# A Fourier factor as four 64x64 tiles of TensorE instead of one block-diagonal 128x128 product

## The chip, the cores and the metric

The kernel runs on one core of one Trainium2 chip. The metric is the device time of one execution in microseconds (us). Most executions agree within 0.3%. Each variant was run several times on a chip beside runs of the kernel before on the same chip. A ratio below is the mean time of a kernel's fast runs over the mean of the other kernel's fast runs of the same rounds, so it isn't quite the ratio of the medians that stand beside it.

Before the change: 3389.97 us (median of three runs, 3387.17 to 3390.71); with the fourth run, which was made beside the changed kernel (3380.72 us), the median is 3388.57 us.

## The reference, cut to what matters

Eight sequences of 3008 tokens with 256 features go through a Fourier filter along the tokens, then each token through a layer of 2048 hidden units with ELU. All in float32.

```python
X = np.fft.rfft(x, axis=1)                 # x: (8, 3008, 256)
Y = X * (filt_r + 1j * filt_i)[None]
y = np.fft.irfft(Y, n=3008, axis=1)
h = y.reshape(24064, 256) @ w_in           # (256, 2048)
g = np.where(h > 0, h, np.exp(np.minimum(h, 0)) - 1)
out = g @ w_out                            # (2048, 256)
```

## The kernel before

3008 = 47 * 64. A token is n = 47 * n2 + n1, and n1 = 24 * h + i with h = 0 or 1. The first factor, a product over n2 (64 values), is done for both halves h at once: h = 0 lies on partitions 0 to 63, h = 1 on 64 to 127, and the table `wa` is block-diagonal, so half of the 128x128 product multiplies by zeros. `psa` is its result in PSUM, `t1` the copy in SBUF (both are on-chip memories), and `z_move` carries `t1` to `t2`, where n1 lies on the partitions. The second factor (`psb`), the filter, and the way back (`psi`, `psn`) follow.

```python
XC = 4                                     # values of i in a chunk; 6 chunks a batch
def a_unit(b, i):                          # two values of i
    c, r = divmod(i, XC // 2)
    ...
    nc.tensor.matmul(ps, wa, xs[b, c][:, 2 * r:2 * r + 2, :], start=True, stop=True)
    nc.scalar.activation(out=t1s[b, c][:, 2 * r:2 * r + 2, :], in_=ps, func=AXT.Copy)

def z_move(b, c):                          # 16 moves of 32 partitions x 1 KB
    ...
    for h in range(2):
        for ri in range(2):
            p0 = h * 64 + ri * 32
            r0 = ri * SL + h * H + c * XC
            for n in range(XC):
                nc.sync.dma_start(t2s[b][r0 + n:r0 + n + 1, :, :], t[p0:p0 + 32, n, :])
```

The layer's work is laid out in slots, 96 a batch. One matmul call leaves two passes in the trace. In each slot TensorE does `up` (4 passes of 512 columns into `ph`) and `down` (8 passes of 256 columns into `po`). The mixing of batch b is put between the slots of batch b - 1: `a_unit` in slots 2, 6, 10 ... 46, `b_unit` from slot 52. Batch 0 is mixed with no layer work beside it; this is the head of the trace.

## Time and profile before

| what | value | view |
|---|---|---|
| span of the profiled run | 3384.2 us | page |
| TensorE busy | 91% | page, engine shares |
| psa | 192 passes, 108.3 us busy | page, groups |
| first pass of the layer (ph) | at 320.0 us | timeline |
| period of a batch (first psb to first psb, mean of six) | 389.3 us | timeline |
| a slot without mixing | 3.44 us | timeline |
| what a psa pair adds to its slot | 0.86 us | timeline |

On TensorE the printed duration of a pass isn't its cost: a psa pass of 592 ns is followed by the next after 429 ns. The cost is the distance from its start to the next start. The lines themselves are shown in the prediction.

### The profile page before, as it was taken

How to read it: one execution, taken by the hardware profiler on the slowest of the kernel's cores; microseconds unless marked ns; L12 is line 12 of the kernel's file. 1: busy time of each engine (PE TensorE's matmuls, PEld its weight loads, DVE VectorE, ACT ScalarE, POOL GpSimd, SP SyncE). 2: the span in 40 equal slices, each digit the busy share in tenths (PEclk: the TensorE clock that was granted, in tenths of full speed). 3: DMA queues.
4: the chain of work that ended last, by engine and by line, in shares of the span. 5: the costliest groups of instructions: out<-in, count | busy, mean ns of one | idle time of the engine just before them, and what ended most of it. 6: DMA issues, size and time to landing. Idle time of an engine off the chain costs nothing.

```text
span 3384.2 us, 30459 instructions
## 1 busy us (share of the span) xinstructions
PE 3075.4 (91%) x11200; PEld 2079.4 (61%) x11200; DVE 1494.1 (44%) x2241; ACT 663.5 (20%) x1137; POOL 171.6 (5%) x148
## 2 busy tenths in 40 slices
PE   1234999999989999999999999899999999999999
PEld 0122666666666666666666666576666666666666
DVE  0185337333553336433473336433373335533343
ACT  0001221222212222222212222122212222122121
POOL 0010002000010001000020001100020000100000
PEclk9656999999999999999999999999999999999999
DMA  7321111102110121101210121102111021100000
GB/s 116 60 82 42 44 36 35 29 19 49 34 37 11 38 43 34 28 17 42 46 34 17 25 48 36 35 13 43 37 35 29 19 50 21 38 10 12 7 13 12
DMA packets 101653, 116.43 MB, mean 34 GB/s; under 512 B 29928, under 2 KB 79848, under 8 KB 101232
## 3 DMA queue, kind: packets, MB, share of 16 engines
q1 hardware_dynamic: 96768, 99.73, 13.9%
q10 hardware_dynamic: 4000, 11.67, 1.3%
q0 software_dynamic: 736, 3.09, 0.8%
q8 instruction: 88, 1.44, 0.2%
q14 instruction: 61, 0.50, 0.1%
HBM read 39.39 MB, written 24.64 MB: 19 GB/s over the span
## 4 chain that ended last, share of the span: by engine, by line
PE 75%; SPq 14%; DMA 7%; DVE 2%; issue 1%; ACT 1%; ACTq 0%; DVEq 0%
PE po L244 34%; PE ph L226 34%; SPq L208 14%; DMA t<-t 4%; PE psn L215 3%; PE psa L158 2%; PE psb L177 1%; DMA wai<-wai_t 1%; PE psi L195 1%; DMA wd<-in_moe_w_out_dram 1%; DMA wd<-in_moe_w_in_dram 0%; SPq L171 0%; DMA out_dram<-o 0%; ACT g L231 0%; ACT t L197 0%
## 5 line engine op out<-in xcount | busy, mean ns | idle before, releaser
L244 PE MATMUL po<-w_out,g 128*128 128x256 f32 x6144 | 1466.0, 382 | 33.8 <-ACT o L248 33.8
L226 PE MATMUL ph<-y,w_in 128*128 128x512 f32 (+1 forms) x3072 | 1425.5, 587 | 32.3 <-DVE g L232 32.2
L244 PEld LDWEIGHTS po<-w_out,g 128*128 128x128 f32 x6144 | 1170.6, 191 | 428.1 <-issue 261.4
L230 DVE TENSOR_SCALAR g<-ph 128x512 f32<-128x512 f32 (+1 forms) x768 | 522.1, 680 | 1040.6 <-PE ph L226 1037.6
L231 ACT ACTIVATE g<-g 128x512 f32<-128x512 f32 (+1 forms) x768 | 475.9, 620 | 2001.2 <-DVE g L230 2001.2
L226 PEld LDWEIGHTS ph<-y,w_in 128*128 128x128 f32 x3072 | 585.5, 191 | 436.4 <-issue 357.0
L232 DVE SCALAR_TENSOR_TENSOR g<-g,ph 128x512 f32<-128x512 f32 (+1 forms) x768 | 519.7, 677 | 665.1 <-ACT g L231 665.1
L188 POOL TENSOR_TENSOR s<-s,s 128x512 f32<-128x512 f32 x128 | 163.9, 1281 | 1237.0 <-DVE s L187 1192.7
L195 PE MATMUL psi<-s,wi 128*96 128x256 f32 x512 | 143.5, 406 | 72.4 <-DVE s L187 50.8
L158 PE MATMUL psa<-xc,wa 128*128 128x512 f32 x192 | 108.3, 655 | 98.6 <-DMA xc<-in_x_dram 98.6
L197 ACT ACTIVATE t<-psi 96x512 f32<-96x512 f32 x128 | 75.4, 589 | 582.0 <-DMA t<-t 499.6
L177 PE MATMUL psb<-t,wb 96*128 96x256 f32 x512 | 142.7, 404 | 44.9 <-DMA t<-t 33.5
L195 PEld LDWEIGHTS psi<-s,wi 128*96 128x96 f32 x512 | 87.9, 174 | 152.7 <-issue 111.7
L183 DVE TENSOR_TENSOR s<-psb,filt 64x512 f32<-64x512 f32 x128 | 86.6, 677 | 147.7 <-PE psb L177 147.2
L177 PEld LDWEIGHTS psb<-t,wb 96*128 96x128 f32 x512 | 103.1, 204 | 74.5 <-issue 47.5
L215 PEld LDWEIGHTS psn<-wai,t 128*128 128x128 f32 x768 | 102.5, 196 | 65.2 <-issue 65.2
L158 PEld LDWEIGHTS psa<-xc,wa 128*128 128x128 f32 x192 | 37.4, 207 | 142.6 <-issue 142.6
L215 PE MATMUL psn<-wai,t 128*128 128x128 f32 x768 | 103.0, 279 | 21.9 <-DMA t<-t 21.9
L187 DVE TENSOR_TENSOR s<-psb,filt 64x512 f32<-64x512 f32 x128 | 89.0, 695 | 1.8
L184 DVE SCALAR_TENSOR_TENSOR s<-psb,filt 64x512 f32<-64x512 f32 x128 | 88.7, 693 | 1.7
L186 DVE TENSOR_TENSOR s<-psb,filt 64x512 f32<-64x512 f32 x128 | 87.5, 684 | 1.7
L146 POOL MEMSET xc<- 64x256 f32 x8 | 2.4, 306 | 1522.3 <-PE psa L158 1450.6
(26 smaller groups left out, 264.3 us busy)
## 6 DMA issues: line engine op xcount, KB each, us to landing
t<-t SPq DMA_DIRECT2D x768, 32.0 KB
t<-t SPq DMA_DIRECT2D x1024, 24.0 KB
out_dram<-o SPq DMA_DIRECT2D x184, 128.0 KB
xc<-in_x_dram SPq DMA_DIRECT2D x88, 256.0 KB
wd<-in_moe_w_in_dram ACTq DMA_DIRECT2D x8, 512.0 KB
wd<-in_moe_w_out_dram ACTq DMA_DIRECT2D x16, 256.0 KB
wb<-wb_t ACTq DMA_DIRECT2D x1, 1536.0 KB
wi<-wi_t ACTq DMA_DIRECT2D x1, 1536.0 KB
```

Source lines behind the costliest of these rows:

```text
L158: nc.tensor.matmul(ps, wa, xs[b, c][:, 2 * r:2 * r + 2, :], start=True, stop=True)
L177: nc.tensor.matmul(ps[:, u, :], wb[:, k, :], t2s[b][:, k, :], start=True, stop=True)
L187: nc.vector.tensor_tensor(out=s2[hi], in0=ps[hi], in1=f[lo], op=ALU.mult)
L188: nc.gpsimd.tensor_tensor(out=s1, in0=s1, in1=s2, op=ALU.add)
L195: nc.tensor.matmul(ps[0:KR, u, :], wi[:, 2 * i + u, :], s[:, u, :], start=True, stop=True)
L208: nc.sync.dma_start(t4s[b][p0 + u:p0 + u + 1, :, :], t[r0:r0 + H, u, :])
L215: nc.tensor.matmul(ps[:, ts(q, P)], t4s[b][:, 4 * m + q, ds(dh * P, P)], wai, start=True, stop=True)
L226: nc.tensor.matmul(ph[:, 0:w], w_in[:, dt, ts(jt, P)], ys[b, m][:, dt, 0:w], start=(dt == 0), stop=(dt == 1))
L230: nc.vector.tensor_scalar(out=g[:, 0:w], in0=ph[:, 0:w], scalar1=0.0, scalar2=None, op0=ALU.min)
L231: nc.scalar.activation(out=g[:, 0:w], in_=g[:, 0:w], func=AXT.Exp)
L232: nc.vector.scalar_tensor_tensor(out=g[:, 0:w], in0=g[:, 0:w], scalar=1.0, in1=ph[:, 0:w], op0=ALU.subtract, op1=ALU.max)
L244: nc.tensor.matmul(po[q // 2][:, q % 2, :], g[:, ts(q, P)], w_out[:, jt, :], start=(jt == 0 and q % 2 == 0), stop=(jt == JT - 1 and q % 2 ...
```

## The change

The intent is to leave out the multiplications by zero. The array is used as four independent tiles of 64x64. A tile takes half h as its rows, and writes to the partitions of g: g = 0 for the first two values of i of the chunk, g = 1 for the other two. The four calls of a chunk go to four different tiles. `t1` is therefore laid out by g on the partitions, and `z_move` reads it so; a_units move from twelve half-visits to six visits a batch.

```diff
-    def a_unit(b, i):
-        c, r = divmod(i, XC // 2)
-        ...
-        ps = psM.tile([P, 2, D], FP32, tag="mx", name="psa")
-        nc.tensor.matmul(ps, wa, xs[b, c][:, 2 * r:2 * r + 2, :], start=True, stop=True)
-        nc.scalar.activation(out=t1s[b, c][:, 2 * r:2 * r + 2, :], in_=ps, func=AXT.Copy)
+    def a_unit(b, c):
+        t1s[b, c] = t1p.tile([P, XC, D], FP32, tag="t1", name="t1")
+        ps = [psM.tile([P, 2, D], FP32, tag="mx", name="psa%d" % h) for h in range(2)]
+        for g in range(2):
+            for h in range(2):
+                r, o = slice(h * 64, h * 64 + 64), slice(g * 64, g * 64 + 64)
+                nc.tensor.matmul(ps[h][o], wa[r, r], xs[b, c][r, 2 * g:2 * g + 2, :], start=True, stop=True)
+        for h in range(2):
+            nc.scalar.activation(out=t1s[b, c][:, 2 * h:2 * h + 2, :], in_=ps[h], func=AXT.Copy)
@@ z_move
-                p0 = h * 64 + ri * 32
-                    nc.sync.dma_start(..., t[p0:p0 + 32, n, :])
+                    p0 = n // 2 * 64 + ri * 32
+                    nc.sync.dma_start(..., t[p0:p0 + 32, 2 * h + n % 2, :])
@@ plan
-            for i in range(2 * NXC):
-                s = t + 2 + 4 * i
+            for c in range(NXC):
+                s = t + 6 + 8 * c
```

(The rest of the diff takes comments out.)

More of the change, by code (lines that the diff above doesn't have):

```diff
@@ L151, in x_load @@
             nc.sync.dma_start(t[h * 64:h * 64 + 64, 0:w, :], rows[:, lo:lo + w, :])
-    def a_unit(b, i):
-        c, r = divmod(i, XC // 2)
-        if r == 0:
-            t1s[b, c] = t1p.tile([P, XC, D], FP32, tag="t1", name="t1")
-        ps = psM.tile([P, 2, D], FP32, tag="mx", name="psa")
-        nc.tensor.matmul(ps, wa, xs[b, c][:, 2 * r:2 * r + 2, :], start=True, stop=True)
-        nc.scalar.activation(out=t1s[b, c][:, 2 * r:2 * r + 2, :], in_=ps, func=AXT.Copy)
+    def a_unit(b, c):
[7 more added lines that the diff above has]
+            nc.scalar.activation(out=t1s[b, c][:, 2 * h:2 * h + 2, :], in_=ps[h], func=AXT.Copy)
     def z_move(b, c):
@@ L167, in z_move @@
             for ri in range(2):
-                p0 = h * 64 + ri * 32
                 r0 = ri * SL + h * H + c * XC
                 for n in range(XC):
-                    nc.sync.dma_start(t2s[b][r0 + n:r0 + n + 1, :, :], t[p0:p0 + 32, n, :])
+                    p0 = n // 2 * 64 + ri * 32
+                    nc.sync.dma_start(t2s[b][r0 + n:r0 + n + 1, :, :], t[p0:p0 + 32, 2 * h + n % 2, :])
     def b_unit(b, i):
@@ L328 @@
             t = (b - 1) * PER
-            for i in range(2 * NXC):
-                s = t + 2 + 4 * i
-                at(s, a_unit, b, i)
-                if i % 2 == 1:
-                    c = i // 2
-                    at(s, z_move, b, c)
-                    nb, nxt = (b, c + 2) if c + 2 < NXC else (b + 1, c + 2 - NXC)
-                    if nb < B:
-                        at(s, x_load, nb, nxt)
+            for c in range(NXC):
+                s = t + 6 + 8 * c
+                at(s, a_unit, b, c)
+                at(s, z_move, b, c)
+                nb, nxt = (b, c + 2) if c + 2 < NXC else (b + 1, c + 2 - NXC)
+                if nb < B:
+                    at(s, x_load, nb, nxt)
             for i in range(NB):
```

## The prediction

> **What bounds the kernel now.** I first read the page: the engine shares, then the chain that ended last.
>
> ```profile
> span 3384.2 us, 30459 instructions
> ...
> PE 3075.4 (91%) x11200; PEld 2079.4 (61%) x11200; DVE 1494.1 (44%) x2241; ACT 663.5 (20%) x1137; POOL 171.6 (5%) x148
> ...
> PEclk9656999999999999999999999999999999999999
> ...
> PE 75%; SPq 14%; DMA 7%; DVE 2%; issue 1%; ACT 1%; ACTq 0%; DVEq 0%
> PE po L244 34%; PE ph L226 34%; SPq L208 14%; DMA t<-t 4%; PE psn L215 3%; PE psa L158 2%; PE psb L177 1%; DMA wai<-wai_t 1%; PE psi L195 1%; DMA wd<-in_moe_w_out_dram 1%; DMA wd<-in_moe_w_in_dram 0%; SPq L171 0%; DMA out_dram<-o 0%; ACT g L231 0%; ACT t L197 0%
> ...
> ```
>
> TensorE bounds it, at 0.9 or more of its clock except in a cold head (the first four slices). The product that changes, psa at L158, is 2% of the chain. But shares over the whole span mix stages, so I asked where psa runs. By stretches: its first 24 records lie in the first 130 us (batch 0, no layer work yet), then 24 records in each of seven stretches of some 165 us, one per batch. For one of these (1105 to 1293 us) I read the waits and TensorE's groups, and then a piece of its timeline.
>
> ```profile
> POOL xc L146 <- PE psa L158: 219.3, 1, 219.3
> ACT g L231 <- DVE g L230: 146.0, 50, 3.6
> ...
> PEld psa L158 <- issue: 4.3, 18, 0.2
> ...
> L158 PE MATMUL psa<-xc,wa 128*128 128x512 f32 x24 | 12.3, 593 | 0.0
> ...
> 1119.42 1.88 PE L226 MATMUL ph<-y,w_in 128*128 128x512 f32 x4
> 1121.14 1.02 PE L158 MATMUL psa<-xc,wa 128*128 128x512 f32 x2
> 1122.00 1.89 PE L244 MATMUL po<-w_out,g 128*128 128x256 f32 x8
> 1123.73 1.88 PE L226 MATMUL ph<-y,w_in 128*128 128x512 f32 x4
> 1125.44 1.89 PE L244 MATMUL po<-w_out,g 128*128 128x256 f32 x8
> ```
>
> The reader is to see three things. No TensorE group idles in this stretch (0.0 before psa), and no wait ends on TensorE waiting for another engine, so a microsecond added or removed there moves the end by a microsecond. Second, one matmul call leaves two records (96 calls, 192 records; weights, pass, weights, pass). Third, the cost of a pass is its distance to the next start, not its printed length: psa takes 1122.00 - 1121.14 = 0.86 us for two, 0.43 us each, while its mean length is 593 ns. The 0.16 us between them is the pipeline's tail, hidden today behind the next pass. The chain of this stretch agrees: it charges 0.86 us to each psa pair.
>
> **What the Trainium skill says.** (1) "TensorEngine Tiling (Array Packing)", section Key Properties: tiles execute independently, but a change of tiling mode drains TensorE. The kernel before shows no such drain: its passes follow each other at 0.43 us, even between products of 96 and 128 rows (psb at 904.72, the next at 905.59). (2) "TensorE: Matmul & The Clock Gate", section "Part 3: Packing small matmuls — row/col tiling": products on different tiles start some 4 ns apart, but matmuls start and end strictly in program order. No run here has tiles yet. (3) The same page, "Back-to-back issue gap", gives N / 2.4 + 2.5 ns, 216 ns for 512 columns; here the measured 0.43 us is twice that, and I use the measurement. (4) The tiling page, "Gotcha 1: PSUM Pressure": different row tiles must not share a bank. The change obeys it (one bank for each half h).
>
> **The change part by part.**
>
> *Removed:* per chunk of four i, two calls of 128x128 by 512 columns: 4 passes x 0.43 = 1.72 us. There are 8 x 6 = 48 chunks, of which 42 (batches 1 to 7) lie in the TensorE-bound stretches: 72 us.
>
> *Added:* per chunk, four calls of 64x64 by 512 columns in the order (h0,g0), (h1,g0), (h0,g1), (h1,g1), each on its own tile: 8 passes of 512 columns. A pass keeps its 512 columns, so I keep 0.43 us for it. The intent is that all four run at once: 2 passes deep, 0.86 us per chunk, half of before.
>
> I doubt that, because of the two passes. Program order is A1 A2 B1 B2 C1 C2 D1 D2, where A2 needs the tile of A1. If starts are in program order (point 2), A2 starts when A1's columns are through, B1 at once beside A2; B2 waits for B1 and C1 goes beside B2; and so on. It is a staircase: five steps, not two: 5 x 0.43 = 2.15 us, 0.43 more than before.
>
> *The two mode switches.* Each chunk goes from the full array to tiles and back, amid layer work. At each, the tail of 0.16 us (593 less 430 ns) is no longer hidden. The first weights of the new mode may also be unable to load ahead; a weight load of 128 columns lasts 190 ns in this trace. So 0.16 to 0.35 us a switch, as an estimate; I take 0.25, 0.5 us per chunk.
>
> *Sum:* 2.15 + 0.5 = 2.65 us against 1.72, so +0.93 us a chunk, times 42 = +39 us.
>
> *Beside other work, so free:* ScalarE's copies stay 96 of some 0.58 us, and two now follow each other; with the exponential of a slot (0.63 us) that is 1.8 us of a 3.44 us slot (1125.44 - 1122.00). They reach across both halves, but the shapes are unchanged. The moves after it keep their count (96 a batch) and size (32 partitions by 1 KB); only the half they read from alternates. The plan moves the even a_units from slots 2, 10, ... to 6, 14, ...; psn at slots 2, 18, 34 no longer shares a slot with psa, which frees nothing on a full TensorE. In the head, psa waits for the DMA of x (98.6 us over six waits) and does not appear on the chain at all; at the cold clock four psa passes span 3.75 us, so an added step is below 1 us, partly hidden: 0 to +2 us. I take 0.
>
> The last move of a batch has room. In this stretch its last issue is at 1283.6 us and the first psb is at 1294.33, some 10 us later. A longer psa delays both alike; a shorter one takes at most 6 x 0.86 = 5 us from the gap. SyncE waits 73.9 us for ScalarE's copies in this stretch, so the queue isn't full either.
>
> So the centre of my leading reading is 3390 + 39 = 3429 us. I shade it by 4 us for the chance that the tiles do better: 3425.
>
> **The rivals.**
>
> *All four tiles at once.* If a blocked second pass holds up only its own tile and not the queue, a chunk takes 0.86 us, plus 0.3 to 0.7 for the switches: 1.2 to 1.6, so -0.5 to -0.1 us a chunk, -21 to -5 us: 3369 to 3385. Even with free switches it is 42 x 0.86 = 36 us, 1.1%, so 2% faster is out of reach. For it: the tiling page calls tiles independent, and the banks are laid out for it. Against: the pair of passes per call, plain in the counts, and the order of starts. Chance 0.25.
>
> *Tiles one after another.* If f32 passes don't overlap across tiles at all, it is 8 x 0.43 = 3.44 us, plus 0.2 to 0.5 for the switches: +1.9 to +2.2 us a chunk, +80 to +92 us: 3470 to 3482, slower by 2.4 to 2.7%. For it: the f32 pass takes twice the skill's figure, so it uses the array or its inputs differently from the case that was measured there. Against: nothing in this trace; it has no tiles. Chance 0.17.
>
> *A staircase with weight loads in it.* Today a pass's weights load during the pass before (the load at 1120.71, its pass at 1121.14). If the load for a new tile can't start until the pass ahead of it in the program starts, each of the three handovers waits for a load of up to 0.19 us: 2.65 + 3 x 0.19 = 3.22 us, +1.5 us a chunk, +63 us: 3453. Chance 0.2; the plain staircase keeps 0.38.
>
> *The end moves to the DMA queue.* If the first factor gets faster, the moves of t1 may end after psb wants them. The 10 us of room speak against it; it would only cut the gain of the first rival.
>
> **Range and chances.** Batches are alike to a few us, so the spread is that of the mechanism, not of the runs (3387 to 3391). The four readings give 3369 to 3482 us. A range of 3370 to 3475 us leaves out the best corner of the first and half of the serial one. 2% faster (3322) is beyond even the free case: 0.01. 2% slower starts at 3458 us: the serial reading, and part of the loaded staircase if its switches cost more than I took: 0.22. Within 2%: 0.77.
>
> **What would show each step.** In the changed profile psa should have 384 records of 64 rows by 512 columns. From the start of the first psa pass to the start of the po pass after it: near 2.6 us for the staircase, 1.2 to 1.6 us for full overlap, 3.6 us or more for none. Within a chunk the eight starts tell it directly: in the staircase, starts come in pairs 0.43 us apart (A2 with B1, B2 with C1, C2 with D1). The switches show as more than 0.43 us from the last ph start to the first psa start, and from the last psa start to the first po. The exact change of the period of a batch (389 us now) times seven should be the change of the time. The prediction is wrong if psa spans 0.9 us (switches free and tiles together), if a TensorE wait for ScalarE's copies or for a psM buffer appears in the stretch, or if psb starts waiting for the moves.

## The result, and the profile after

The changed kernel takes 3368.38 us (median of four, 3365.12 to 3369.85); the ratio to the kernel before is 0.994 (95% interval 0.9926 to 0.9954). It is 20 us faster than the median of all four runs before, where the prediction had 35 us slower; the time lies 1.6 us under the range on record.

From the page of the changed kernel (the span, the engine shares and the groups of the new product):

```profile
span 3366.1 us, 30866 instructions
...
PE 3058.7 (91%) x11392; PEld 2050.8 (61%) x11392; DVE 1495.1 (44%) x2241; ACT 663.2 (20%) x1137; POOL 171.8 (5%) x148
...
L160 PE MATMUL psa<-xc,wa 64*64 64x512 f32 x384 | 69.2, 673 | 100.4 <-DMA xc<-in_x_dram 100.4
...
L160 PEld LDWEIGHTS psa<-xc,wa 64*64 64x64 f32 x384 | 12.3, 140 | 150.5 <-issue 127.8
...
```

The group of the old product on the page before:

```profile
L158 PE MATMUL psa<-xc,wa 128*128 128x512 f32 x192 | 108.3, 655 | 98.6 <-DMA xc<-in_x_dram 98.6
```

There are twice the passes of psa (384), and yet they keep TensorE busy for less time, 69.2 us against 108.3 us. A pass lasts no less (673 ns, before 655 ns), so the passes must lie side by side.

The timeline of TensorE in a stretch of the TensorE-bound stage (start, duration, line, product, number of passes):

```profile
1115.18 1.88 PE L229 MATMUL ph<-y,w_in 128*128 128x512 f32 x4
1116.99 1.09 PE L160 MATMUL psa<-xc,wa 64*64 64x512 f32 x8
1118.01 1.99 PE L247 MATMUL po<-w_out,g 128*128 128x256 f32 x8
1119.84 0.59 PE L229 MATMUL ph<-y,w_in 128*128 128x512 f32 x1
```

The slot with psa lasts 1119.84 - 1115.18 = 4.66 us (the same in all 42 such slots), a slot without 3.44 to 3.45 us. A chunk thus costs 1.21 us, against 2 x 0.86 = 1.72 us before: 0.51 us saved, times 42 chunks of batches 1 to 7 = 21 us. Eight passes take 1.02 us to the start of po. The same view up to 1117.1 us has four of them:

```profile
1116.99 0.66 PE L160 MATMUL psa<-xc,wa 64*64 64x512 f32 x4
```

Record by record in the packed trace, the eight starts are four at 1116.992, 1116.999, 1117.005 and 1117.012, and four at 1117.472 to 1117.492. All four tiles work together, twice; the experiments below test this reading.

In the same stage the waits (who waited for whom; us in total, times, longest) are as before: none of TensorE's own matmuls waits for another engine.

```profile
POOL xc L146 <- PE psa L160: 216.7, 1, 216.7
ACT g L234 <- DVE g L233: 142.9, 50, 3.2
...
PEld psa L160 <- issue: 4.5, 6, 0.8
...
```

The 18.1 us between the two profiled runs fall as follows, from the first starts of products in both traces.

| stretch | before, us | after, us | difference |
|---|---|---|---|
| start to the first ph (head) | 320.0 | 324.5 | +4.5 |
| first ph to the first psb of batch 1 | 195.4 | 192.5 | -2.9 |
| from there to the first psb of batch 7 (six batches) | 2335.8 | 2314.6 | -21.2 |
| from there to the last start | 527.8 | 529.3 | +1.5 |

The seven stages with psa give -24.1 us; psa itself gives 21 of them. As to the rest, TensorE's idle time before ph fell from 32.3 to 28.2 us; why was not followed up. The head's +4.5 us is taken up below.

### The profile page after: what moved, and what is told of

The parts are those of the page before. It is cut to its first block, busy times and chain, and to the rows that moved or that the text cites. A ratio compares the mean times of both kernels' runs of the same rounds, so it can differ in the third digit from the quotient of the medians.

```text
span 3366.1 us, 30866 instructions
## 1 busy us (share of the span) xinstructions
PE 3058.7 (91%) x11392; PEld 2050.8 (61%) x11392; DVE 1495.1 (44%) x2241; ACT 663.2 (20%) x1137; POOL 171.8 (5%) x148
## 4 chain that ended last, share of the span: by engine, by line
PE 74%; SPq 15%; DMA 6%; DVE 2%; issue 1%; ACT 1%; ACTq 0%; POOL 0%; DVEq 0%; POOLq 0%
PE po L247 34%; PE ph L229 33%; SPq L211 15%; DMA t<-t 4%; PE psn L218 3%; PE psb L180 1%; PE psa L160 1%; DMA wai<-wai_t 1%; PE psi L198 1%; DMA wd<-in_moe_w_out_dram 1%; DMA wd<-in_moe_w_in_dram 0%; SPq L174 0%; DMA out_dram<-o 0%; ACT g L234 0%; ACT t L200 0%
## 5 line engine op out<-in xcount | busy, mean ns | idle before, releaser
L229 PE MATMUL ph<-y,w_in 128*128 128x512 f32 (+1 forms) x3072 | 1428.3, 587 | 28.2 <-DVE g L235 28.2
L160 PE MATMUL psa<-xc,wa 64*64 64x512 f32 x384 | 69.2, 673 | 100.4 <-DMA xc<-in_x_dram 100.4
L160 PEld LDWEIGHTS psa<-xc,wa 64*64 64x64 f32 x384 | 12.3, 140 | 150.5 <-issue 127.8
```

What stands on the lines that cost most here:

```text
L160: nc.tensor.matmul(ps[h][o], wa[r, r], xs[b, c][r, 2 * g:2 * g + 2, :], start=True, stop=True)
L229: nc.tensor.matmul(ph[:, 0:w], w_in[:, dt, ts(jt, P)], ys[b, m][:, dt, 0:w], start=(dt == 0), stop=(dt == 1))
```

## The experiments

All kernels gave the reference's result. The table has the medians and the ratios to the kernel before; the runs of it on the same chip had medians of 3383.15 us (first four rows), 3385.53 us (next three), 3386.5 us (next four) and 3386.7 us (last three). The medians of before_again and before_look count one slow run each; their fast runs alone have 3388.67 and 3385.25 us.

| run | median, us | ratio (95%) |
|---|---|---|
| before_again | 3389.72 | 1.0016 (1.0001 to 1.0031) |
| after_again | 3363.52 | 0.9939 (0.9925 to 0.9952) |
| split_same | 3366.43 | 0.9949 (0.9935 to 0.9963) |
| split_turn | 3365.75 | 0.9946 (0.9933 to 0.996) |
| switch_twice | 3380.16 | 0.9985 (0.9971 to 0.9999) |
| paired | 3356.14 | 0.9909 (0.9896 to 0.9923) |
| moves_by_source | 3350.83 | 0.9894 (0.9881 to 0.9908) |
| before_look | 3385.43 | 0.9998 (0.9984 to 1.0013) |
| before_moves | 3370.63 | 0.9953 (0.9942 to 0.9965) |
| moves_far | 3323.41 | 0.9815 (0.9802 to 0.9828) |
| paired_moves | 3344.43 | 0.9878 (0.9866 to 0.9891) |
| two_tiles | 3399.61 | 1.0045 (1.003 to 1.0059) |
| before_far | 3344.61 | 0.9884 (0.987 to 0.9898) |
| paired_far | 3318.27 | 0.9801 (0.9789 to 0.9814) |

### Controls: before_again, after_again, before_look

No edit. Expected of before_again:

> The unchanged kernel before against itself: the noise of the ratio, and a second profile of its head. All theories: ratio 1.000 within 0.3%. If the head's end is a matter of the program, its first ph pass starts at 320 us again (within 1 us); if it is scatter of the DMA, it moves by several us, and then the 4.6 us by which the changed kernel's first ph starts later (324.5) is no part of the change.

Expected of after_again:

> The changed kernel unchanged, as the control of this call. All theories: 0.994 of the kernel before, 0.992 to 0.996. Its first ph pass at 324.5 us again if the later head belongs to the change, anywhere from 318 to 326 if it is scatter.

Expected of before_look:

> The unchanged kernel again, for a profile of its head in the fast state (the last one fell into a state four times slower). Changed kernels so far had their first ph at 320.8 to 324.5 us, the kernel before at 320.0 once. If the head is not of the change, this one lies between 318 and 325 as well; if the change costs the head some 2 us, it is at 320 or below. Time ratio 1.000 within 0.3%.

The changed kernel repeats its gain (0.9939). Its first ph pass came at 320.9 us this time, not 324.5: most of the later head of the first profile is scatter. The other variants with one of the two old orders of moves have it at 320.8 to 322.3 us. The kernel before has one fast profile of its head (320.0 us), and a loss of 1 or 2 us there isn't excluded. The ratio of before_again is 0.16% off 1, so differences under 0.2% are not read below.

### Does a pass that waits for its tile hold up the others? split_same, split_turn

The prediction's staircase rests on this. In split_same each call of 512 columns becomes two calls of 256 on the same tile, one right behind the other; in split_turn the same eight calls take turns over the tiles.

```diff
+                for u in range(2):            # split_same: inside g, h
-                nc.tensor.matmul(ps[h][o], wa[r, r], xs[b, c][r, 2 * g:2 * g + 2, :], ...)
+                    nc.tensor.matmul(ps[h][o, u, :], wa[r, r], xs[b, c][r, 2 * g + u, :], ...)
```

```diff
+        for u in range(2):                    # split_turn: outside g, h
```

> The changed kernel, with each tile's 512 columns in two calls of 256 right behind each other, so that in the program every second call needs a tile that is busy. Theory 1 (a pass that waits for its tile is passed by later passes for free tiles): four rounds of 0.215 us, 0.86 us as now, chunk 1.0 to 1.1 us from the first psa start to po; time that of the changed kernel within 0.3% (3368, up to 3376 with a few hundredths more per round). Theory 2 (only the two passes of one call are laid apart, a call that waits for its tile holds up the calls behind it, the staircase of the prediction one level up): ten steps of 0.215 us, 2.15 us, +1.29 us a chunk over 42 chunks: +54 us, 3422.

> The same eight calls of 256 columns, but taking turns: four tiles, then the four tiles again. Theory 1 and theory 2 alike: no call waits for a tile behind which others could go, 0.86 us of rounds, time of the changed kernel within 0.3%. If this is as slow as split_same, the cost is of the number of calls, not of their order.

Both run at the time of the changed kernel (0.9949 and 0.9946 against 0.9939). The timeline of TensorE in split_same:

```profile
1114.12 1.88 PE L230 MATMUL ph<-y,w_in 128*128 128x512 f32 x4
1115.93 1.11 PE L161 MATMUL psa<-xc,wa 64*64 64x256 f32 x16
1116.98 1.99 PE L248 MATMUL po<-w_out,g 128*128 128x256 f32 x8
1118.81 1.88 PE L230 MATMUL ph<-y,w_in 128*128 128x512 f32 x4
```

Sixteen passes in 1.05 us to po, and 1118.81 - 1114.12 = 4.69 us for the slot, 0.03 us more than with four calls. A staircase of ten steps, with whole calls kept in order, would have shown 2.15 us; with single passes kept in order it is thirteen steps, 2.80 us. Record by record, the starts come in four rounds of four, 0.22 to 0.27 us apart. So later calls pass over calls that wait for a tile. In split_same the first pass for the fourth tile has twelve passes ahead of it in the program; three of them had started on the other tiles, and nine were passed over. The price is small: starts within a round are 13 ns apart, and 7 ns in split_turn.

The head of the changed kernel shows the same in another way. There the second half of x comes late. Three views of TensorE's timeline, up to 9.4 us, 13.3 to 13.5 us, and 14.25 to 14.4 us:

```profile
8.43 1.94 PE L160 MATMUL psa<-xc,wa 64*64 64x512 f32 x2 [8.43 <-DMA xc<-in_x_dram]
...
13.40 1.12 PE L160 MATMUL psa<-xc,wa 64*64 64x512 f32 x3 [3.04 <-DMA xc<-in_x_dram]
...
13.40 1.98 PE L160 MATMUL psa<-xc,wa 64*64 64x512 f32 x6 [3.04 <-DMA xc<-in_x_dram]
```

Both passes of the first call run alone at 8.43 us (0.88 us apart; the kernel before has 0.85 us in its head, at a granted clock of 0.50 from 97 to 102 us). The second call needs the other half of x, and everything waits for it, also the third call, whose data is there: a wait for data holds up the queue. When it ends at 13.40 us, three passes start within 13 ns, and the last three 0.91 us later. No fixed order of the eight starts explains both this and the stage above. Here the second pass of the first call ran before the first pass of the second call; there four tiles started before any second pass. The records don't name their tile; but the two passes of one call were 0.88 us apart where they ran alone, so three that start within 13 ns are on three tiles. Which unit deals the passes out isn't in the trace.

### Passes on one tile: two_tiles

The upper left and the lower right tile alone do all the work, two calls each, in the program order h = 0, 0, 1, 1. The layout and the moves are those of the kernel before, with four banks and four copies a chunk.

```diff
-        for g in range(2):
-            for h in range(2):
-                r, o = ...
-                nc.tensor.matmul(ps[h][o], wa[r, r], xs[b, c][r, 2 * g:2 * g + 2, :], ...)
+        for h in range(2):
+            r = slice(h * 64, h * 64 + 64)
+            ps = [psM.tile([P, 2, D], FP32, tag="mx", ...) for g in range(2)]
+            for g in range(2):
+                nc.tensor.matmul(ps[g][r], wa[r, r], xs[b, c][r, 2 * g:2 * g + 2, :], ...)
+            for g in range(2):
+                nc.scalar.activation(out=t1s[b, c][r, 2 * g:2 * g + 2, :], in_=ps[g][r], ...)
```

> The same products on two tiles alone (upper left and lower right), two calls one after the other on each, program order h0, h0, h1, h1, four banks and four copies of 64 partitions a chunk; layout and moves of the kernel before. Theory (a visit costs the passes that fall on one tile, 0.43 us each, plus 0.35 us): 4 x 0.43 + 0.35 = 2.07 us a chunk, +0.86 us over 42 chunks: +36 us against the changed kernel, 3400 to 3404, slower than the kernel before by 14. If the strict order of starts of my prediction held, h1 would start only beside the second h0 call: six steps, 2.93 us, 3438. If the two tiles shared a limit of f32 streaming: eight steps, 3474.

```profile
1122.27 1.88 PE L229 MATMUL ph<-y,w_in 128*128 128x512 f32 x4
1124.08 1.94 PE L160 MATMUL psa<-xc,wa 64*64 64x512 f32 x8
1125.95 1.99 PE L247 MATMUL po<-w_out,g 128*128 128x256 f32 x8
1127.78 0.59 PE L229 MATMUL ph<-y,w_in 128*128 128x512 f32 x1
```

This is TensorE's timeline again. The slot lasts 5.51 us, so a chunk costs 2.07 us, as worked out from four passes of 0.43 us on each tile. The time, 3399.61 us, is at the low end of where this theory put it. With whole calls kept in order a chunk would have cost 2.93 us, six steps; with single passes in order, as the prediction had it, it is seven steps, 3.36 us (the expectation counts six). The packed records also mark the passes that end a call: the pair at 1124.562 and 1124.575 us does, so it is the second passes of the first and the third call, and the third call had started both its passes before the second call started its first (1124.99 us). The same tables and the same zeros left out, but on two tiles, lose 0.45% against the block-diagonal product. The gain of the change is the working together of four tiles.

### What a visit to the tiles costs: switch_twice, paired

In switch_twice each chunk is done in two visits four slots apart, 256 columns on four tiles each time; the copies stay together. In paired two chunks are done in one visit, in slots 6, 22 and 38.

```diff
-                at(s, a_unit, b, c)
+                at(s - 4, a_unit, b, c, 0)    # switch_twice: ps[h][o, u, :] for u = 0
+                at(s, a_unit, b, c, 1)        # then u = 1 and the copies
```

```diff
-            for c in range(NXC):
-                s = t + 6 + 8 * c
+            for c2 in range(0, NXC, 2):       # paired
+                s = t + 6 + 8 * c2
+                for c in (c2, c2 + 1):
+                    at(s, a_unit, b, c)
+                for c in (c2, c2 + 1):
+                    at(s, z_move, b, c)       # and x_load as before
```

> The changed kernel with each chunk's columns in two visits four slots apart (four tiles of 256 columns each time): the streamed columns stay, the mode switches double. Theory (what keeps the chunk at 1.21 us instead of 0.86 is paid per visit: 0.09 us going in, 0.09 us and 0.10 us coming out, 0.05 us between the rounds): +0.28 to +0.35 us a chunk over 42 chunks, +12 to +15 us against the changed kernel, 3380 to 3383. Rival (it is paid per streamed column, passes in tiles being slower): no difference, 3368 within 3 us. My prediction's own 0.25 us a switch would make it +21 us.

> The changed kernel with two chunks in one visit (slots 6, 22, 38), half as many switches. Theory of a cost per visit: 3 visits fewer a batch, 21 in batches 1 to 7, 0.28 to 0.35 us each: -6 to -7 us, 3361 to 3362. Rival per column: no difference. Rival that the moves come late (32 moves at once, all four psM buffers taken): psb or psn waits, slower than 3368.

TensorE's timeline, first of switch_twice, then of paired:

```profile
1117.36 1.88 PE L233 MATMUL ph<-y,w_in 128*128 128x512 f32 x4
1119.17 0.66 PE L162 MATMUL psa<-xc,wa 64*64 64x256 f32 x8
1119.76 1.99 PE L251 MATMUL po<-w_out,g 128*128 128x256 f32 x8
1121.59 1.88 PE L233 MATMUL ph<-y,w_in 128*128 128x512 f32 x4
```

```profile
1109.94 1.88 PE L229 MATMUL ph<-y,w_in 128*128 128x512 f32 x4
1111.75 1.95 PE L160 MATMUL psa<-xc,wa 64*64 64x512 f32 x16
1113.62 1.99 PE L247 MATMUL po<-w_out,g 128*128 128x256 f32 x8
1115.46 1.88 PE L229 MATMUL ph<-y,w_in 128*128 128x512 f32 x4
```

Take the slot's 3.44 to 3.45 us and the columns (0.215 us for 256, 0.43 us for 512, times the passes on one tile) from the distance of the ph starts:

- switch_twice: 4.23 - 3.445 - 2 x 0.215 = 0.355 us a visit.
- changed kernel: 4.66 - 3.445 - 2 x 0.43 = 0.355 us a visit.
- paired: 5.52 - 3.445 - 4 x 0.43 = 0.355 us a visit.
- two_tiles: 5.51 - 3.445 - 4 x 0.43 = 0.345 us a visit, with two tiles only.
- kernel before: 4.30 - 3.445 - 2 x 0.43 = about 0 us, with no tiles.

The cost is paid per visit, not per column or per tile. That it is a drain at the change of mode is the likely reading; no run shows the drain itself. In the changed kernel it lies at four places, from the starts of the records: 0.09 us before the first psa pass, 0.05 us between the two rounds, 0.09 us before the first po pass, and 0.10 us between the first two po passes (0.32 us apart, where it is 0.215 us elsewhere); the 0.02 us left are the starts of one round, 7 ns apart. The times follow: switch_twice is 0.46% slower than the changed kernel's control, some 16 us (expected 12 to 15), and paired is 0.3% faster, some 10 us (expected 6 to 7; the last few us aren't certain). In the traces the seven stages with psa are 8 us shorter than in the changed kernel.

### The moves on the way: moves_by_source, before_moves, moves_far, paired_moves, before_far, paired_far

These began as a test of the head. The changed kernel reads `t1` from alternating halves of the partitions; moves_by_source groups the moves by source again, and so changes the order of the destinations too.

```diff
-        for h in range(2):
-            for ri in range(2):
-                for n in range(XC):           # n = 2 * g + (0, 1)
+        for g in range(2):                    # moves_by_source
+            for ri in range(2):
+                for h in range(2):
+                    for n in range(2):        # row 2 * g + n
```

> The changed kernel with its 16 moves of a chunk issued by source partitions again (four from one quarter, then the next), as in the kernel before; destinations in another order. If the order of the sources makes the head later (first ph at 324.5 against 320.0), the head ends near 320 and the time is 4 to 5 us lower, 3364. If the head's end is scatter or comes from elsewhere, no difference, 3368 within 3 us.

It was faster by far more than expected: the ratio 0.9894, first ph at 305.8 us. Since the head had only scattered, this couldn't be the undoing of a loss by the change. Either the constant source helps, or the order of the destinations. before_moves gives the kernel before this order of destinations, with a source that changes every two moves. moves_far has neither neighbour:

```diff
+        for n in range(XC):                   # moves_far, before_far
+            for ri in range(2):
+                for h in range(2):            # destination row ri * 48 + h * 24 + 4 * c + n
```

> The kernel before with the destinations of its moves in the order of moves_by_source (two neighbouring rows of t2, then two 24 rows on), while its source quarter changes every two moves. Theory D (neighbouring destination rows in one after another slow the moves): the head shrinks as there, first ph near 306, 15 us less than the kernel before: ratio 0.995 to 0.996. Theory S (only a constant source quarter over four moves helps, here it is lost): no gain or a loss, ratio 1.000 to 1.003. In either case this part has nothing to do with the tiles.

> The changed kernel with moves whose destination jumps by 24 or 48 rows every time and whose source quarter changes at least every second move. Theory D: as fast as moves_by_source (3351) or better by a few us, first ph at 306 or below. Theory S: as slow as the changed kernel, 3364 to 3368, first ph at 321.

> Two chunks in one visit and the moves in the order of moves_by_source together. If the two gains are of different places (switches on TensorE in batches 1 to 7; moves in the head), they add up: 3351 less 7 to 10, 3341 to 3344, ratio 0.986 to 0.988. If the late moves of a pair meet psb (room of 5.6 us in the changed kernel), less.

> The kernel before (128x128 product) with the far order of moves. If the 43 us that the far order gains in the changed kernel are a matter of the moves alone: 3386 less 40 to 45, 3341 to 3346, ratio 0.987 to 0.988, and the tiles are worth 18 to 22 us on top of it. If they needed the tiles: less.

> Two chunks a visit and the far order of moves: the best of all. If the gains add: 3323 less 7 to 10, 3313 to 3317, ratio 0.979 to 0.980. In the head only the moves bind, so its first ph stays at 280.

The timeline of SyncE's queue in the head (start, duration of the whole group, number of DMA issues), first of the changed kernel, then of moves_far:

```profile
74.47 19.63 SPq L174 DMA_DIRECT2D t<-t  x16
94.20 1.18 SPq L151 DMA_DIRECT2D xc<-in_x_dram  x2
95.84 18.16 SPq L174 DMA_DIRECT2D t<-t  x16
```

```profile
66.48 10.05 SPq L174 DMA_DIRECT2D t<-t  x16
76.63 1.18 SPq L151 DMA_DIRECT2D xc<-in_x_dram  x2
77.91 10.35 SPq L174 DMA_DIRECT2D t<-t  x16
```

In the far order 16 issues take 10.05 us, 0.63 us each, hardly over the 0.59 us of one issue: the queue hardly waits for moves to land any more. From 50 to 140 us the queue's waits of z_move for moves fall from 35.9 us to 6.9 us. The lines, from 50 to 140 us (us in total, times, longest), first of the changed kernel, then of moves_far:

```profile
SPq L174 <- DMA t<-t: 35.9, 32, 4.7
```

```profile
SPq L174 <- DMA t<-t: 6.9, 3, 5.7
```

The first ph comes at 280.2 us instead of 321 to 324, and the time is 3323.41 us where 3351 us or a few us less was expected. before_far gains the same on the kernel before (0.9884, first ph at 279.7 us), so this has nothing to do with the tiles. before_moves gained as well (0.9953), so it is the order of the destinations; a constant source isn't needed.

The Trainium skill has a reason that fits: "SBUF — State Buffer", section "Door 1: The DMA port swizzle", says that four neighbouring partitions share a port. The four rows of a chunk (24 * h + 48 * ri + 4 * c + n) are four such partitions, and before the change and after it they were written one after another. Four in a row took 13.0 to 19.6 us for 16 moves in the two profiles, two in a row 11.4 to 16.0 us, one alone 10.05 to 11.5 us (chunks 1 to 5 of batch 0). No run told ports apart from mere distance between rows.

The gains add up nearly: paired_far, at 3318.27 us (ratio 0.9801), is faster than both kernels. It was expected at 3313 to 3317 us; its gain over moves_far is 0.14%, under the 0.2% that is read here, and so is that of paired_moves (3344.43 us, expected 3341 to 3344) over moves_by_source, 0.16%. The traces settle it: through pairing the seven stages with psa became 8 us shorter in paired, 9 us in paired_moves and 7 us in paired_far, and the visits alone explain 21 x 0.355 = 7.5 us.

## Why the prediction was wrong, point by point

- **TensorE's time moves the end one to one in the stretches with psa.** Right. psa was worked out from the slots to save 21 us, and the seven stages became 24.1 us shorter; 3 us of this are open. In two_tiles psa costs 42 x 0.85 = 36 us more than in the changed kernel, and the stages are 36 us longer.
- **A pass of 512 columns keeps its 0.43 us.** Right: 0.48 us between the rounds of one visit, of which 0.05 us is paid once a visit; the third and fourth pass on a tile cost 0.43 us each (two_tiles, paired).
- **The staircase.** This step failed, in the words "if starts are in program order (point 2), A2 starts when A1's columns are through, B1 at once beside A2". The runs show that a pass which waits for its tile is passed by passes for free tiles. A visit costs the passes on one tile: two in the changed kernel (0.86 us), four in two_tiles (1.72 us), not five steps of the queue (2.15 us). The prediction took a page's statement about the order of starts for a case that no trace of this kernel had shown, two passes a call on tiles, and gave the contrary only 0.25.
- **The two switches, 0.5 us a chunk.** Right in kind, too large: 0.355 us a visit, everything counted. Where 0.16 us of hidden tail was charged at each switch, the first start after it comes 0.09 us late.
- **The sum.** 2.65 us was predicted for a chunk and 1.21 us measured. 1.29 us of the difference is the staircase and 0.15 us the switches.
- **What lies beside is free.** Right: no wait for copies or psM buffers appears. The last move of a batch was issued 5.6 us before psb (1282.3 and 1287.95 us), not 10 us any more. The prediction allowed for 5 us less, but for another reason, so that the size agrees is luck: it had psb come sooner through a shorter psa. In the traces psb follows the last psa pass by 22.9 us before and 23.1 us after, while the last move's issue follows it by 12.1 us before and 17.4 us after.
- **The head, 0 us.** Right within its scatter: first ph at 320.8 to 324.5 us in the changed kernel and the variants that keep its moves, 320.0 us in the one profile of the kernel before; with the far moves 280.2 us with tiles and 279.7 us without.
- **The rivals.** "All four tiles at once" gave 1.2 to 1.6 us a chunk and 3369 to 3385 us; measured are 1.21 us and 3368 us, its best corner. The range left that corner out on purpose, and so missed the result by 1.6 us. "Tiles one after another" and the loaded staircase fell with split_same and two_tiles. Faster by 2% was rightly called out of reach of this change.

## What to carry to other kernels

When a product has structural zeros, tiles of the array can remove them, but what a visit costs is the number of passes on the busiest tile plus a fixed price of a visit to the tiles and back, 0.355 us here; so use all tiles at once, and do as much as the banks allow in one visit. Before relying on an order of execution that a page states, ask whether it was measured with your kind of call, and look in the head or at a late operand for starts that give the order away. And look at the queue's waits in a head that waits for moves: the order of 16 small moves was worth twice the whole change.

## What the Trainium skill lacked or had wrong

- "TensorE: Matmul & The Clock Gate", section "Part 3: Packing small matmuls — row/col tiling", says that matmuls start and end strictly in program order. For f32 calls, which leave two passes each, passes for a free tile start before earlier passes that wait for their tile: eight passes of four calls in two rounds of four, 7 ns apart within a round and 0.48 us between rounds; in split_same nine waiting passes were passed over. A wait for data does hold up the calls behind it (13.40 us in the head).
- "TensorEngine Tiling (Array Packing)", section Key Properties, says that a change of mode drains TensorE, without a figure: 0.355 us for a visit there and back, in three kernels, and 0.345 us with two tiles.
- "TensorE: Matmul & The Clock Gate", section "Back-to-back issue gap", has no figure for f32: a call of 512 columns leaves two passes of 0.43 us, 0.86 us in all, four times the 0.216 us of its formula. Its section on LDWEIGHTS gives the columns over 1.2, so 107 ns for 128 and 53 ns for 64; the trace prints 190 ns and 129 to 133 ns. These are printed durations, not distances: four loads for four tiles start 7 ns apart.
- "SBUF — State Buffer", section "Door 1: The DMA port swizzle", explains ports within one DMA. A cost of moves inside one core to neighbouring single partitions, issued one after another, is on no page that was read: 13.0 to 19.6 us for 16 moves against 10.05 to 11.5 us in another order. Whether the port is the reason stays open.
